# Decay times v as three wide bf16 matmuls per head, summed from three PSUM slots

## The chip, the cores and the metric

The kernel runs on one core of a Trainium2 chip. The metric is device time in microseconds, the median of several runs of one kernel. The profile is of one further execution, whose span runs from the first to the last instruction.

## The reference

An mLSTM over 4 batches, 8 heads, 768 steps and head size 40, followed by a gated feed-forward. For each batch and head:

```python
m_new = max(f + m, i);  f_stab = exp(f + m - m_new);  i_stab = exp(i - m_new)
C = f_stab * C + i_stab * outer(v, k);   n = f_stab * n + i_stab * k
h = C @ q;   y = sigmoid(o) * h / max(abs(n . q), 1)
```

and then, with `x` of shape 3072 x 320 and 1536 hidden columns: `out = (sigmoid(x @ w_gate) * (x @ w_val)) @ w_out`. All inputs and outputs are float32.

## The kernel before, in words

The 768 steps are cut into 6 chunks of 128. A **unit** is one chunk of one batch (8 heads), so there are 24 units, 4 to a chunk; chunk 2 begins with unit 8. In a unit, `d` is the 128 x 128 decay matrix of each head. The scores `s` (q times k, L753) are multiplied into it on VectorE (`t`, L872), so that `d` then holds decay times score. `av` (L931) multiplies it by `v`, to which a column of ones is added, so that 41 columns give the 40 outputs and the denominator. `in` (L914) gives the contribution of the carried state `cst`, scaled by `ti` (L919). `ad` (L946) adds the two in PSUM, `nd` (L951 to L953) makes the reciprocal of the denominator from the 41st column, `ns` (L957) multiplies by the output gate, `ro` (L962) divides, `tx` (L971) transposes in blocks, and `xw`, `xr` bounce the unit's rows through DRAM (`scx`) to `xf`, transposed. `xh` and `xl` (L1000, L1004) split them into a high and a low part, the input of the feed-forward. `cs`, `cm`, `cd`, `ca` carry the state on.

From chunk 2 on (`halved`), `d` and `v` are split into three bf16 parts each: the upper half of the float32 word (`top`), the upper half of the remainder, and the remainder of that. GpSimd makes them: `da`, `db` for `d` (L887, L891) and `va`, `vb` for `v` (L898, L902). `av` is six matmuls of 41 columns per head, for the six products that matter, all added into one PSUM tile of 8 x 41 columns.

The feed-forward of a chunk runs over 12 blocks of 128 hidden columns, some of them in two halves of two batches. Of a block, `u0`, `r0` fill one PSUM bank (gate) and `u1`, `r1` another (value); `th` (ScalarE), `gx` (VectorE, into the value's bank), `gh` (ScalarE) and `gl` (VectorE, L1097) make the product's high and low part; `dn` multiplies by `w_out`. The next block's `u1` needs the bank that `gl` reads.

PSUM has eight banks: two for the feed-forward's blocks, four for its outputs, and two (`pa`) that all attention tiles take in turn. The program order is a list written out by hand, `ORDER`: each engine, and the queue of SP that issues nearly all DMAs, does its instructions in the list's order.

The masks `bmask` and `cmask` (128 x 3 x 128 and 128 x 3 x 41) tell which rows belong to which of three stacked heads; `rmask` is one column of `bmask`.

Of the kernel before, what the change touches and what calls it, by code (L numbers as in the profile page):

```python
# [23 lines left out]
    'AV': 2,  # L24
# [7 lines left out]
    'AD': 1,  # L32
# [15 lines left out]
    i2 lf wdr0 li i3 wz tab wk0 war0 pz wk1 wk2 wk3 wdo0 ga i0 gm0 il sp0.0 lq2 i1 wdv0 gs0 wbr0 gb wao0 wbo0 lq0  # L48
    wav0 lk0 gc tap tac sp0.1 ee0.0 lk1 gm1 sp1.0 wco0 lq1 wcr0 ee0.1 kw0 lo0 tr0.1 wor0 whr0 wbv0 wlr0 gm2 lv0 i5
# [38 lines left out]
    gh23 u0.24 sh9.1 ns8 r0.24 th24 gl23 dn22.1 u1.24 r1.24 u0.25 nd8 r0.25 sl9.1 gx24 s9.2 th25 s9.1 cd8.1 t9.2
    gh24 dn23.0 s9.0 gl24 tw10.2 u0.26 tw10.0 ro8 r0.26 t9.0 tw10.3 u1.25 r1.25 ea10 t9.1 gx25 sq10.0 dn23.1 gh25
    cs8 tx8 th26 sr10.00 sr10.01 sr10.02 cm8.1 cm8.0 lk11 sr10.10 sr10.11 sr10.12 xw8.3 dn24.0 xw8.2 dn24.1 gl25  # L90
    u1.26 r1.26 gx26 lv10 u0.28 og9 r0.28 va9 dn25.1 gh26 vb9 ob0.2 dn25.0 th28 gl26 u1.28 r1.28 da9 gx28 lv11
    dn26.1 gh28 sh10.0 u0.27 r0.27 tq11 gl28 xw8.1 tw11.3 sl10.0 tw11.1 ca8.1 dn26.0 dn28.2 tw11.2 u1.27 r1.27 th27
    sh10.1 ee10 in9 gx27 tw11.0 db9 av9.0 av9.1 sq10.1 av9.2 sl10.1 u0.29 r0.29 ld11 dn28.3 gh27 gl27 cd8.0 ti9 l110
    va10 th29 ad9 nd9 sq11.0 ns9 u1.29 r1.29 l111 sq11.1 gx29 gh29 dn27.1 lo10 xw8.0 s10.2 u0.30 dn27.0 em10 kw10
    ro9 s10.0 t10.2 s10.1 sr11.00 sr11.01 sr11.02 sr11.10 sr11.12 r0.30 gl29 t10.1 dn29.2 t10.0 u1.30 th30 da10 db10
    r1.30 in10 u0.31 cd10.1 cd10.0 dn29.3 gx30 gh30 r0.31 th31 sr11.11 cs9 lk12 cm9.1 vb10 gl30 ca8.0 u1.31 r1.31
    gx31 dn30.2 gh31 ld12 gl31 dn30.3 og10 u0.32 tx9 xw9.0 xw9.1 xw9.2 r0.32 ti10 th32 sh11.0 xr8.0 u1.32 xr8.2
    r1.32 ea11 dn31.3 gx32 gh32 gl32 u0.34 dn31.2 r0.34 tq12 lq13 tw12.3 tw12.0 tw12.1 cm9.0 tw12.2 u1.34 lo11 xw9.3
    r1.34 dn32.3 th34 gx34 u0.33 va11 r0.33 dn32.2 ee11 em11 gh34 gl34 u1.33 sh11.1 r1.33 ob1.1 sl11.0 lv12 th33
    gx33 av10.0 ld13 sl11.1 av10.1 av10.2 u0.35 xr8.1 kw11 r0.35 gh33 cd9.1 og11 gl33 ad10 xr9.0 ns10 cd9.0 s11.2  # L100
    t11.2 dn33.3 dn33.2 nd10 u1.35 r1.35 s11.0 dn34.3 t11.0 lq15 vb11 th35 gx35 dn34.2 gh35 ro10 cs10 lk13 xr9.2
    s11.1 sr12.10 ca9.1 u0.36 sr12.00 ea12 r0.36 ee12 em12 cm10.1 th36 gl35 u1.36 ca9.0 t11.1 da11 tx10 xw10.1
    xw10.2 r1.36 xw10.3 xw10.0 db11 sr12.02 gx36 dn35.2 cm10.0 kw12 gh36 xr9.1 gl36 sq12.0 u0.37 r0.37 tq13 dn35.3
    dn36.3 u1.37 sr12.11 r1.37 sr12.01 in11 ca10.0 av11.0 av11.1 av11.2 th37 u0.38 gx37 gh37 sr12.12 gl37 ti11 ad11
    r0.38 u1.38 th38 r1.38 nd11 dn36.2 gx38 gh38 ns11 dn37.3 ea13 xh8 ro11 gl38 u0.39 r0.39 tw13.0 xh9 dn37.2 tw13.3
    tx11 xw11.3 xw11.2 xw11.0 xw11.1 u1.39 cd11.1 r1.39 xl8 xr10.0 xl9 xr10.2 th39 xr10.1 dn38.2 gx39 tw13.1 gh39
    gl39 dn38.3 u0.40 r0.40 lo12 ca10.1 xr11.0 sh12.0 dn39.3 sl12.0 u1.40 r1.40 tw13.2 xr11.2 dn39.2 xr11.1 th40
    gx40 sh12.1 ob1.3 gh40 u0.41 ob1.0 cs11 gl40 r0.41 th41 dn40.1 cm11.0 cm11.1 sl12.1 u1.41 r1.41 gx41 u0.42 r0.42
    s12.2 lo13 s12.1 l112 va12 ld14 gh41 gl41 th42 dn41.1 u1.42 r1.42 xh10 xl10 xh11 t12.2 gx42 s12.0 lq14 dn40.0
    dn41.0 gh42 xl11 vb12 ee13 og12 sq12.1 u0.43 r0.43 th43 lk14 og13 sr13.10 sr13.11 sq13.0 sr13.12 sq13.1 cd11.0  # L110
    t12.1 gl42 u1.43 r1.43 dn42.1 dn42.0 ob1.2 t12.0 da12 db12 gx43 gh43 gl43 u0.44 r0.44 u1.44 r1.44 th44 gx44
    dn43.2 u0.45 sr13.00 sr13.02 sr13.01 gh44 em13 r0.45 in12 av12.0 av12.1 sh13.1 kw13 tq14 tw14.1 av12.2 gl44
    u1.45 th45 ti12 dn44.2 cd12.0 tw14.3 r1.45 cd12.1 ca11.0 ad12 dn43.3 dn44.3 nd12 sl13.1 u0.46 r0.46 sh13.0 gx45
    ns12 in13 tw14.0 ld15 lv13 gh45 ca11.1 gl45 cs12 tw14.2 ro12 tx12 cd13.1 xw12.1 sl13.0 xw12.2 dn45.3 ti13 xw12.3
    cm12.0 u1.46 s13.2 cd13.0 t13.2 th46 lk15 r1.46 l113 gx46 dn45.2 xw12.0 cm12.1 sq14.0 s13.1 lv15 lv14 va13 vb13
    s13.0 sr14.00 sr14.01 sr14.02 sr14.10 sr14.11 gh46 l114 t13.1 t13.0 gl46 ca12.0 u0.47 r0.47 sr14.12 u1.47 r1.47
    ea15 ee15 cs13 lo15 sq14.1 th47 av13.0 gx47 gh47 ea14 dn46.0 ee14 ca12.1 gl47 cm13.0 ca13.0 dn46.1 tq15 lq17
    lk16 sh14.0 u0.48 r0.48 sl14.0 th48 dn46.2 dn47.2 em15 lo14 u1.48 sh14.1 u0.49 sl14.1 r1.48 r0.49 dn47.1 da13
    cm13.1 db13 ld16 lq16 tw15.0 dn46.3 tw15.1 dn47.3 dn47.0 tw15.2 gx48 s14.0 gh48 gl48 av13.1 av13.2 ad13 em14
    ns13 kw14 dn48.1 nd13 t14.0 u1.49 th49 ro13 tw15.3 tx13 ca13.1 l115 xr12.0 s14.2 ea16 ee16 dn48.2 dn48.0 s14.1  # L120
    sr15.10 t14.2 og14 r1.49 gx49 u0.50 r0.50 t14.1 gh49 sr15.12 gl49 sr15.00 og15 tq16 va15 sr15.11 in14 ti14 th50
# [1040 lines left out]
```

## Time and profile before

| | |
|---|---|
| runs | 518.97 us median of 3 (517.19 to 519.06) |
| profiled execution, span | 517.4 us, 1.6 us below that median |
| TensorE busy | 506.7 us, 4020 instructions |
| VectorE, ScalarE, GpSimd busy | 332.8, 242.1, 246.3 us |
| granted TensorE clock | 1.000 over the span |
| DMA | 74.17 MB, mean 143 GB/s |

The span is what the instructions take from the first to the last; a run's time is taken by the device around it. Matmuls are pipelined: a record's length is not its cost, and the cost of a row of equal matmuls is read from the chain of waits, which gives each piece the time that it adds.

### The profile page before, as it was taken

The numbers are of one execution on the slowest core, as the hardware profiler recorded it, in microseconds if no ns is written. First come the engines' busy times: TensorE is split into PE (matmuls) and PEld (weight loads), VectorE is DVE, ScalarE is ACT, GpSimd is POOL, SyncE is SP. The second block draws the span as 40 slices with busy tenths as digits, with TensorE's granted clock in tenths as the row PEclk, the third lists the DMA queues.
The fourth block names the chain that finished last, engine by engine and source line by source line (L and its number), as shares of the span: only waits on it lengthen the run. The fifth ranks groups of instructions, "written<-read, shape, count | busy, mean of one in ns | idle before, by whom it ended". The sixth has DMA issues, their size and how long they took to land.

```text
span 517.4 us, 11006 instructions
## 1 busy us (share of the span) xinstructions
PE 506.7 (98%) x4020; PEld 468.3 (91%) x4021; DVE 332.8 (64%) x699; ACT 242.1 (47%) x560; POOL 246.3 (48%) x272
## 2 busy tenths in 40 slices
PE   6989999999999999999999999999999999999997
PEld 4789988889999999998888888898888888999996
DVE  7978877785776677678766456856445474642332
ACT  4887766554444354644444443353344324232322
POOL 3656546557146686459536544187315504510000
PEclk9999999999999999999999999999999999999999
DMA  8999875339687797799879787599465835220000
GB/s 196 259 231 225 223 201 141 102 95 178 135 185 156 166 203 163 162 205 158 171 138 178 181 153 141 135 181 185 96 146 102 173 81 111 65 58 1 1 27 27
DMA packets 222478, 74.17 MB, mean 143 GB/s; under 512 B 167380, under 2 KB 214168, under 8 KB 222424
## 3 DMA queue, kind: packets, MB, share of 16 engines
q1 hardware_dynamic: 221336, 73.20, 64.8%
q8 instruction: 32, 0.52, 0.4%
q10 hardware_dynamic: 1088, 0.26, 0.2%
q14 instruction: 22, 0.18, 0.1%
HBM read 61.54 MB, written 11.90 MB: 142 GB/s over the span
## 4 chain that ended last, share of the span: by engine, by line
PE 89%; DMA 5%; ACT 2%; DVE 2%; issue 1%; SPq 1%; POOL 0%; POOLq 0%; DVEq 0%; ACTq 0%
PE pg L1070 38%; PE po L1107 8%; PE po L1109 8%; PE po L1108 7%; PE pg L1074 6%; PE pg L1075 6%; PE av L931 3%; PE s L753 2%; PE av L938 2%; DMA d<-mscr 2%; PE in L914 2%; PE cs L1014 2%; PE s L808 1%; DMA st_v<-in_moe_w_val_dram 1%; DMA scx<-tx 1%
## 5 line engine op out<-in xcount | busy, mean ns | idle before, releaser
L1092 ACT ACTIVATE gh<-pg 128x256 fp32r<-128x256 f32 (+1 forms) x103 | 48.2, 468 | 142.9 <-DVE pg L1087 120.7
L1087 DVE SCALAR_TENSOR_TENSOR pg<-sg,pg 128x256 f32<-128x256 f32 (+1 forms) x103 | 54.8, 532 | 92.1 <-PE pg L1075 75.4
L1070 PE MATMUL pg<-xh,wh 128*128 128x256 f32 (+1 forms) x412 | 104.8, 336 | 0.2 <-ACT xh L1000 0.2
L1070 PE MATMUL pg<-xh,wl 128*128 128x256 f32 (+1 forms) x412 | 100.9, 326 | 0.0
L1070 PE MATMUL pg<-xl,wh 128*128 128x256 f32 (+1 forms) x412 | 100.8, 326 | 0.0
L1107 PE MATMUL po<-oh,gh 128*128 128x320 f32 x288 | 92.6, 322 | 0.0
L1109 PE MATMUL po<-oh,gl 128*128 128x320 f32 x288 | 89.1, 309 | 0.1
L1108 PE MATMUL po<-ol,gh 128*128 128x320 f32 x288 | 88.9, 309 | 0.0
L1080 ACT ACTIVATE sg<-pg 128x256 f32<-128x256 f32 (+1 forms) x103 | 48.1, 467 | 73.3 <-PE pg L1075 71.9
L1097 DVE TENSOR_TENSOR gl<-pg,gh 128x256 fp32r<-128x256 f32 (+1 forms) x103 | 54.3, 527 | 36.6 <-ACT gh L1092 34.9
L1070 PEld LDWEIGHTS pg<-xl,wh 128*128 128x128 f32 x412 | 69.1, 189 | 7.3 <-POOL xl L1004 0.3
L1070 PEld LDWEIGHTS pg<-xh,wl 128*128 128x128 f32 x412 | 69.0, 189 | 7.1
L1070 PEld LDWEIGHTS pg<-xh,wh 128*128 128x128 f32 x412 | 67.7, 189 | 3.7 <-DVE gl L1097 0.6
L1074 PE MATMUL pg<-xh,w 128*128 128x256 f32 (+1 forms) x206 | 68.5, 333 | 0.0
L1075 PE MATMUL pg<-xl,w 128*128 128x256 f32 (+1 forms) x206 | 67.0, 326 | 0.0
L1107 PEld LDWEIGHTS po<-oh,gh 128*128 128x128 f32 x288 | 54.4, 189 | 2.5
L1108 PEld LDWEIGHTS po<-ol,gh 128*128 128x128 f32 x288 | 54.2, 188 | 2.6
L1109 PEld LDWEIGHTS po<-oh,gl 128*128 128x128 f32 x288 | 54.1, 188 | 0.7 <-DVE gl L1097 0.6
L671 POOL TENSOR_SCALAR_AFFINE_SELECT d<-d 128x1024 f32<-128x1024 f32 x22 | 26.2, 1192 | 52.6 <-ACT d L667 51.9
L887 POOL TENSOR_TENSOR dr<-d 128x1024 f32<-128x1024 f32 x16 | 30.3, 1894 | 35.7 <-DVE d L872 35.3
L872 DVE TENSOR_TENSOR d<-s,d 128x384 f32<-128x384 f32 (+2 forms) x68 | 34.9, 527 | 14.5 <-PE s L753 8.9
L1075 PEld LDWEIGHTS pg<-xl,w 128*128 128x128 f32 x206 | 39.0, 189 | 2.7
(159 smaller groups left out, 886.2 us busy)
## 6 DMA issues: line engine op xcount, KB each, us to landing
d<-mscr SPq DMA_DIRECT2D x22, 512.0 KB
ks<-scq SPq DMA_DIRECT2D x48, 168.0 KB
qs<-scq SPq DMA_DIRECT2D x48, 168.0 KB
scq<-tq SPq DMA_DIRECT2D x64, 80.0 KB
su_o<-in_moe_w_out_dram SPq DMA_DIRECT2D x12, 320.0 KB
o<-in_o_gate_dram SPq DMA_DIRECT2D x24, 160.0 KB
v<-in_v_dram SPq DMA_DIRECT2D x24, 160.0 KB
out_dram<-ob SPq DMA_DIRECT2D x24, 160.0 KB
```

Of the source, the lines that this page charges most:

```text
L872: nc.vector.tensor_tensor(y, ps_[n, g][:, :nh, :], y, ALU.mult)
L887: E("da", n).tensor_tensor(dr[n][0], dm[n], top(dm[n]), ALU.subtract)
L1070: nc.tensor.matmul(p, w[y][:, a, fs], x[c][:, a, n0:n1], start=(i + a == 0), stop=False)
L1074: nc.tensor.matmul(pg[n, y], w2[y][:, fs], xh[c][:, 2, n0:n1], start=False, stop=False)
L1075: nc.tensor.matmul(pg[n, y], w2[y][:, fs], xl[c][:, 2, n0:n1], start=False, stop=True)
L1080: nc.scalar.activation(s, pg[n, 0], AF.Tanh, scale=0.5)
L1087: nc.vector.scalar_tensor_tensor(sgs[n], gate, 1.0, pg[n, 1], ALU.add, ALU.mult)
L1092: nc.scalar.activation(ghs[n][:, :nt], sgs[n], AF.Copy)
L1097: E("gl", n).tensor_tensor(gls[n][:, :nt], sgs[n], ghs[n][:, :nt].bitcast(F32), ALU.subtract)
L1107: nc.tensor.matmul(p, ghs[n][:, ts], oh[:, j, :], start=(j == 0), stop=False)
L1108: nc.tensor.matmul(p, ghs[n][:, ts], ol[:, j, :], start=False, stop=False)
L1109: nc.tensor.matmul(p, gls[n][:, ts], oh[:, j, :], start=False, stop=(j == NF - 1))
```

## The change

From chunk 2 on, `v`'s three bf16 parts lie side by side in one tile `vs` (slots of 41 columns), and a head's product is three matmuls: the top of `d` times all three parts (123 columns), the last remainder of `d` times the first part (41), and the middle part of `d` times the first two (82). The slots stay apart in PSUM, so a unit's product is two tiles of four heads (`av{n}.0`, `av{n}.1`, one bank each), and VectorE adds the state's contribution and the three slots (`ad{n}.{half}{slot}`). `nd` and `ns` run for each half. A ScalarE copy `vc` puts the top of `v` into the tile; `va`, `vb` write into its other slots. Scores and their products go in two groups of four heads instead of 3, 3 and 2. The large masks are dropped for `rmask`, which is now made directly; the product with a mask reads it broadcast; `cd` scales all 120 rows of the state, whose unused rows `iz` clears at the start.

The order of feed-forward instructions on TensorE, ScalarE and VectorE is the same. SP's order is the same but for `ld16`, which now stands between the third and the last `tw` of unit 15, after four steps that stood behind it. Attention steps stand at other places, as here around the products of units 18 and 19:

```diff
-    ... u0.64 xr17.1 cm17.0 s19.2 t19.2 s19.1 t19.1
-    dn62.2 r0.64 gh63 db18 s19.0 t19.0 th64 av18.0 vb19 lo21 av18.1 av18.2 xr16.1 gl63 sr20.10 dn63.0 sr20.12 u1.64
-    r1.64 u0.65 da19 db19 ad18 r0.65 lq21 sr20.11 xh16 og19 cd18.0 nd18 ns18 ro18 in19 av19.0 av19.1 tx18 xw18.2
-    xw18.0 xw18.1 xw18.3 xl16 av19.2 ld20 dn63.1 gx64 gh64 th65 gl64 u1.65 r1.65 u0.66 r0.66 dn63.3 dn63.2 dn64.2
-    cd18.1 xh17 ti19 dn64.1 sr20.00 sr20.01 og21 sr20.02 cd17.1 dn64.3 xl17 ad19 nd19 ns19 ro19 tx19 gx65 gh65 th66
+    ... u0.64 s19.0 s19.1 xr17.1 db18 dn62.2 va18 vb18
+    cd18.1 r0.64 gh63 t19.0 av18.1 t19.1 th64 lo21 av18.0 xr16.1 gl63 vc19 sr20.10 dn63.0 sr20.12 va19 da19 u1.64
+    cd18.0 ad18.10 ad18.11 ad18.00 ad18.01 ad18.12 r1.64 ad18.02 u0.65 r0.65 nd18.1 ns18.1 lq21 nd18.0 ns18.0 ro18
+    sr20.11 xh16 tx18 in19 og19 xw18.2 xw18.0 xw18.1 vb19 xw18.3 db19 xl16 ld20 dn63.1 gx64 av19.0 ti19 gh64 th65
+    av19.1 gl64 u1.65 r1.65 u0.66 ad19.00 ad19.10 r0.66 dn63.3 cd17.1 ad19.01 ad19.11 dn63.2 dn64.2 ad19.12 ad19.02
+    xh17 ns19.0 dn64.1 sr20.00 sr20.01 og21 sr20.02 nd19.0 ns19.1 dn64.3 xl17 nd19.1 cs18 ro19 tx19 gx65 ca17.1 gh65
```

The code, cut to its core:

```diff
+FOURS = ((0, 4), (4, 4))
...
-    bmask = const.tile([P, 3, L], F32, name="bmask")
-    cmask = const.tile([P, 3, DA], F32, name="cmask")
-    ones = bmask[:BH, 0, :]
+    ones = rmask[:BH, 0:1].broadcast_to([BH, L])
...
+    @op("iz")
+    def _():
+        nc.gpsimd.memset(cst[64:, :, 2, : 2 * DA], 0.0)
...
-        block_mask(bmask, L)
+        block_mask(rmask.unsqueeze(2), 1)
...
-                for g, (h0, nh) in enumerate(GROUPS):
+                for g, (h0, nh) in enumerate(FOURS):
                     @op(f"s{n}.{g}")
...
+            @op(f"vc{n}")
+            def _():
+                vs[n] = sbt("su", [P, H, 3, DA], F32, f"vs_{n}", 2)
+                nc.scalar.activation(top(vs[n][:, :, 0, :]), top(vt[n]), AF.Copy)
...
-                E("va", n).tensor_tensor(vr[n][0], vt[n], top(vt[n]), ALU.subtract)
+                E("va", n).tensor_tensor(vs[n][:, :, 1, :], vt[n], top(vt[n]), ALU.subtract)
...
-            for i in range(3):
-                @op(f"av{n}.{i}")
-                def _(i=i):
-                    if i == 0:
-                        pv_[n] = pst(P_(f"av{n}"), [P, H, DA], f"av_{n}")
-                    dp = top(dm[n]) if i == 0 else top(dr[n][0]) if i == 1 else dr[n][1]
-                    vp = [top(vt[n])] if i == 2 else [top(vt[n]), top(vr[n][0]), vr[n][1]][: 3 - i]
-                    for h in range(H):
-                        for j, w in enumerate(vp):
-                            nc.tensor.matmul(pv_[n][:, h, :], dp[:, h, :], w[:, h, :], start=(i + j + h == 0),
-                                             stop=(i == 2 and h == H - 1))
+            for y in range(2):
+                @op(f"av{n}.{y}")
+                def _(y=y):
+                    pv_[n, y] = p = pst("pa", [P, 4, 3, DA], f"av_{n}_{y}")
+                    parts = vs[n].rearrange("p h j e -> p h (j e)").bitcast(BF16)
+                    for i, (dp, w) in enumerate(((top(dm[n]), 3 * DA), (dr[n][1], DA), (top(dr[n][0]), 2 * DA))):
+                        for x in range(4):
+                            nc.tensor.matmul(p.rearrange("p x j e -> p x (j e)")[:, x, :w], dp[:, 4 * y + x, :],
+                                             parts[:, 4 * y + x, 1 : 2 * w : 2], start=(i + x == 0), stop=(i + x == 5))
+
+                for i in range(3):
+                    @op(f"ad{n}.{y}{i}")
+                    def _(y=y, i=i):
+                        if n not in t1s:
+                            t1s[n] = sbt("t1", [P, H, DA], F32, f"t1_{n}", 2)
+                        t, p = t1s[n][:, 4 * y : 4 * y + 4, :], pv_[n, y][:, :, i, :]
+                        if c == 0 and i == 0:
+                            nc.scalar.activation(t, p, AF.Copy)
+                        else:
+                            nc.vector.tensor_tensor(p if i == 2 else t, t, p, ALU.add)
...
+        for y in range(2 if halved else 1):
+            hs = (lambda y=y: pv_[n, y][:, :, 2, :]) if halved else lambda: pv_[n]
+            heads = slice(4 * y, 4 * y + 4) if halved else slice(0, H)
```

## Rows read from the trace of the kernel before

**Rows 1.** The page's busy table: us busy, share of the span, instructions.
```profile
PE 506.7 (98%) x4020; PEld 468.3 (91%) x4021; DVE 332.8 (64%) x699; ACT 242.1 (47%) x560; POOL 246.3 (48%) x272
```

**Rows 2.** Busy time by stages: stretch, its length, each engine's us and instructions.
```profile
230.00:256.00 26.00, 25.97 (x188) 22.76 (x187) 21.22 (x34) 12.53 (x25) 18.58 (x19) 1.00 0.89 162
...
312.00:359.00 47.00, 46.87 (x423) 41.76 (x422) 33.98 (x65) 18.11 (x32) 27.25 (x26) 1.00 0.79 157
...
430.00:460.00 30.00, 30.00 (x291) 28.87 (x290) 17.18 (x37) 11.39 (x23) 12.24 (x11) 1.00 0.29 67
```

**Rows 3.** TensorE's waits from 300 us on: waiter, releaser, us, times, longest.
```profile
PE pg L1070 <- ACT xh L1000: 0.2, 1, 0.2
```

**Rows 4.** The chain of waits: start, us that it adds, work, matmuls.
```profile
262.33 1.21 PE av L931 x48
...
318.18 1.39 PE pg L1070 x6
...
332.86 0.29 PE s L753 x3
...
452.70 0.72 PE pg L1070 x6
```

**Rows 5.** Groups by line and shape, VectorE: count, busy us, mean ns, idle before.
```profile
L957 DVE SCALAR_TENSOR_TENSOR o<-o,av 128x320 f32<-128x320 f32 x24 | 11.2, 465 | 1.2 <-ACT o L906 0.4 <-PE av L938 0.4
L946 DVE TENSOR_TENSOR av<-t,av 128x328 f32<-128x328 f32 x20 | 10.0, 500 | 3.9 <-PE av L931 3.4 <-PE av L938 0.2
...
L872 DVE TENSOR_TENSOR d<-s,d 128x256 f32<-128x256 f32 x20 | 8.4, 419 | 6.8 <-PE s L753 5.5 <-PE s L808 1.2
...
L872 DVE TENSOR_TENSOR d<-s,d 128x512 f32<-128x512 f32 x8 | 5.1, 683 | 0.1
L953 DVE RECIPROCAL den<-den 128x8 f32<-128x8 f32 x24 | 4.9, 203 | 0.8
...
L952 DVE SCALAR_TENSOR_TENSOR den<-av,den 128x8 f32<-128x8 f32 x24 | 4.0, 166 | 0.8
...
L951 DVE TENSOR_SCALAR den<-av 128x8 f32<-128x8 f32 x24 | 3.8, 160 | 0.3
```

**Rows 6.** The same groups, ScalarE, the output gates.
```profile
L906 ACT ACTIVATE o<-o 128x320 f32<-128x320 f32 x24 | 10.9, 464 | 2.9 <-DMA o<-in_o_gate_dram 2.9
```

**Rows 7.** The same groups, GpSimd, the last remainder of the decay.
```profile
L891 POOL TENSOR_TENSOR ds<-dr 128x1024 bf16<-128x1024 f32 x16 | 30.6, 1915 | 0.9
```

**Rows 8.** Instructions in order of time from 0 us, VectorE's first scan.
```profile
3.42 0.45 DVE L409 TENSOR_TENSOR_SCAN gin<-bmask,gin 32x128 f32<-32x128 f32 x1 [0.56 <-DMA gin<-in_f_gate_dram]
```

**Rows 9.** The chain of waits into the start of chunk 4.
```profile
359.96 5.09 DMA scx<-tx
...
366.16 2.05 DMA xf<-scx
...
368.24 0.53 ACT xh L1000
...
368.81 1.83 PE pg L1070 x6
```

**Rows 10.** VectorE in order of time, 346 to 359 us: start, us, [idle before].
```profile
346.96 0.89 DVE L872 TENSOR_TENSOR d<-s,d 128x256 f32<-128x256 f32 x2 [1.73 <-PE s L753]
348.46 0.56 DVE L872 TENSOR_TENSOR d<-s,d 128x384 f32<-128x384 f32 x1 [0.61 <-PE s L753]
...
353.63 0.69 DVE L1097 TENSOR_TENSOR gl<-pg,gh 128x512 fp32r<-128x512 f32 x1 [0.67 <-ACT gh L1092]
...
355.72 0.50 DVE L946 TENSOR_TENSOR av<-t,av 128x328 f32<-128x328 f32 x1 [0.71 <-PE av L931]
...
357.78 0.51 DVE L971 STREAM_TRANSPOSE tx<-x 128x320 f32<-128x320 f32 x1
```

**Rows 11.** Groups by line and shape, TensorE's weight loads of scores and decay.
```profile
L753 PEld LDWEIGHTS s<-qs,ks 126*128 126x128 f32 x128 | 18.5, 190 | 1.3 <-DVE t L919 0.5
...
L931 PEld LDWEIGHTS <-d 128*128 128x128 bf16 x384 | 11.7, 98 | 0.4 <-issue 0.3
```

More of the change, by code (lines that the diff above doesn't have):

```diff
@@ L23 @@
     'V32': 1,
-    'AV': 2,
+    'AVN': 8,
     'EP': (),
@@ L88 @@
[L88 to L97, printed above, removed]
@@ new lines @@
+    ob1.0 gl40 r0.41 th41 dn40.1 sl12.1 u1.41 r1.41 gx41 cm11.0 u0.42 r0.42 lo13 s12.1 l112 ld14 gh41 gl41 th42
+    dn41.1 u1.42 r1.42 xh10 xl10 ca11.0 vc12 xh11 gx42 s12.0 lq14 dn40.0 dn41.0 gh42 xl11 t12.1 t12.0 ee13 og12
+    sq12.1 u0.43 va12 r0.43 th43 da12 lk14 og13 sr13.10 sr13.11 sq13.0 sr13.12 vb12 sq13.1 gl42 u1.43 ca11.1 db12
+    r1.43 dn42.1 dn42.0 in12 ob1.2 gx43 gh43 gl43 u0.44 r0.44 u1.44 r1.44 av12.0 th44 ti12 av12.1 gx44 dn43.2 u0.45
+    sr13.00 sr13.02 sr13.01 gh44 em13 r0.45 sh13.1 kw13 tq14 tw14.1 gl44 u1.45 ad12.00 ad12.10 ad12.01 cd12.0
@@ L560, in mlstm_then_gated_ffn_kernel @@
     pt_, ps_, pi_, pv_, px_, pc_, pm_ = {}, {}, {}, {}, {}, {}, {}
-    split, vr, dr, stk, sgn, tx, xf = {}, {}, {}, {}, {}, {}, {}
+    split, vs, dr, stk, sgn, tx, xf = {}, {}, {}, {}, {}, {}, {}
     POPEN = {
@@ L798, in _ @@
                 @op(f"qb{n}.{g}")
-                def _(g=g, nh=nh, r=r):
+                def _(g=g, h0=h0, nh=nh, r=r):
                     qkt, qbd = sop[n]
-                    E(f"qb{g}", n).tensor_tensor(qbd[:r, g, :nh, :], qkt[:r, g, 0, :].unsqueeze(1).broadcast_to([r, nh, L]),
-                                                 bmask[:r, :nh, :], ALU.mult)
+                    E(f"qb{g}", n).tensor_tensor(qbd[:r, h0 : h0 + nh, :], qkt[:r, g, 0, :].unsqueeze(1).broadcast_to([r, nh, L]),
+                                                 rmask[:r, :nh].unsqueeze(2).broadcast_to([r, nh, L]), ALU.mult)
                 @op(f"s{n}.{g}")
-                def _(g=g, nh=nh, r=r):
+                def _(g=g, h0=h0, nh=nh, r=r):
                     qkt, qbd = sop[n]
                     ps_[n, g] = p = pst(P_(f"s{n}.{g}"), [P, 3, L], f"s_{n}_{g}")
-                    nc.tensor.matmul(p[:, :nh, :], qkt[:r, g, 1, :], qbd[:r, g, :nh, :], start=True, stop=True)
+                    nc.tensor.matmul(p[:, :nh, :], qkt[:r, g, 1, :], qbd[:r, h0 : h0 + nh, :], start=True, stop=True)
         else:
@@ L866, in _ @@
                                               sc[:, 0, :, x, :].rearrange("m d w -> d m w"))
-        for g, (h0, nh) in enumerate(((0, 4), (1, 4)) if padded or paired else GROUPS):
+        for g, (h0, nh) in enumerate(((0, 4), (1, 4)) if padded or paired else FOURS if bounced else GROUPS):
             @op(f"t{n}.{g}")
@@ L938, in _ @@
                     nc.tensor.matmul(p[:, h, :], dm[n][:, h, :], vt[n][:, h, :], start=True, stop=True)
-        def hs():
-            return t1s[n] if c > 0 and not PARAM["AD"] else pv_[n]
-        if c > 0:
+        if c > 0 and not halved:
             @op(f"ad{n}")
             def _():
-                nc.vector.tensor_tensor(hs(), t1s[n], pv_[n], ALU.add)
-        @op(f"nd{n}")
-        def _():
-            rden[n] = den = sbt("den", [P, H], F32, f"den_{n}", 2)
-            nc.vector.tensor_scalar(den, hs()[:, :, D], -2.0, 2.0, ALU.mult, ALU.max)
-            nc.vector.scalar_tensor_tensor(den, hs()[:, :, D], 2.0, den, ALU.mult, ALU.max)
-            nc.vector.reciprocal(den, den)
-        @op(f"ns{n}")
-        def _():
-            nc.vector.scalar_tensor_tensor(ot[n], ot[n], 1.0, hs()[:, :, :D], ALU.add, ALU.mult)
+                nc.vector.tensor_tensor(pv_[n], t1s[n], pv_[n], ALU.add)
+        for y in range(2 if halved else 1):
+            hs = (lambda y=y: pv_[n, y][:, :, 2, :]) if halved else lambda: pv_[n]
+            heads = slice(4 * y, 4 * y + 4) if halved else slice(0, H)
+            yn = f"{n}.{y}" if halved else f"{n}"
+            @op(f"nd{yn}")
+            def _(hs=hs, heads=heads):
+                if n not in rden:
+                    rden[n] = sbt("den", [P, H], F32, f"den_{n}", 2)
+                den = rden[n][:, heads]
+                nc.vector.tensor_scalar(den, hs()[:, :, D], -2.0, 2.0, ALU.mult, ALU.max)
+                nc.vector.scalar_tensor_tensor(den, hs()[:, :, D], 2.0, den, ALU.mult, ALU.max)
+                nc.vector.reciprocal(den, den)
+            @op(f"ns{yn}")
+            def _(hs=hs, heads=heads):
+                o = ot[n][:, heads, :]
+                nc.vector.scalar_tensor_tensor(o, o, 1.0, hs()[:, :, :D], ALU.add, ALU.mult)
         @op(f"ro{n}")
@@ L1039, in _ @@
                 tmps[y] = tmp
-                if is_act("cm", n):
-                    for j in range(w // DA):
-                        js = slice(j * DA, (j + 1) * DA)
-                        nc.scalar.activation(tmp[:, :, js], pc_[n][:r, gs, js], AF.Copy, scale=rmask[:r, j : j + 1])
-                else:
-                    cm = cmask.rearrange("p j e -> p (j e)")[:r, :w].unsqueeze(1).broadcast_to([r, ng, w])
-                    nc.vector.tensor_tensor(tmp, pc_[n][:r, gs, :w], cm, ALU.mult)
+                for j in range(w // DA):
+                    js = slice(j * DA, (j + 1) * DA)
+                    nc.scalar.activation(tmp[:, :, js], pc_[n][:r, gs, js], AF.Copy, scale=rmask[:r, j : j + 1])
             if c > 0:
```

220 lines of the change are left out of this document (111 added, 109 removed).

## The prediction

> **What bounds the kernel now.** I read the page's busy table first: TensorE is busy 506.7 us, 98% of the span of 517.4 us [rows 1]. So the time is TensorE's own work plus the places where it waits. The table by stages comes next, because the change loads VectorE: VectorE is busy 21.22 of 26.00 us at 230 to 256 us and 33.98 of 47.00 us at 312 to 359 us, while TensorE has next to no idle time in either [rows 2]. The third view, TensorE's waits, has a single one after 300 us: the first matmul of a chunk waited for `xh` [rows 3]. The chain of waits shows where that one comes from, and I return to it below. A TensorE microsecond saved therefore shows only as long as no such wait takes it back.
>
> The profiled execution spans 517.4 us and the timed runs have a median of 518.97 us (517.19 to 519.06), 1.6 us above it. I sum against the span and move the median by the result.
>
> **The change, part by part.** Sixteen units (8 to 23, chunks 2 to 5) change.
>
> *Matmuls of decay times v.* A unit issues 48 bf16 matmuls of 41 columns now. The chain gives 1.21 us for the 48 of one unit, 25.2 ns each [rows 4]. After the change it issues 24: per head one of 123 columns, one of 82 and one of 41. The column count is the same (8 x 246 = 48 x 41 = 1968), so only what a matmul costs beyond its columns can go. Six 512-column matmuls take 1.39 us and six 256-column ones 0.72 us [rows 4], which is 232 and 120 ns each, so 0.436 ns a column and 8 ns fixed. With the fixed part, 123 columns cost 62 ns and 82 cost 44; without it 54 and 36. The 41-column one keeps 25. A head costs 115 to 131 ns against 6 x 25.2 = 151, so 20 to 36 ns are saved. I take the middle, 28 ns: 8 heads give 0.225 us a unit, 16 units 3.6 us, with ends 2.6 and 4.6 us.
>
> The Trainium skill ("TensorE: Matmul & The Clock Gate", Wait — 56ns, not 53.3ns?) states that spacing never falls below about 25 ns however few the columns, and is columns / 2.4 plus 2.5 ns otherwise; the 25.2 ns row agrees. By that rule 123, 82 and 41 columns cost 54, 37 and 25 ns, which is the upper end of the saving, 4.6 us.
>
> *VectorE's sums.* Each half unit of four heads now holds three slots, and VectorE adds them: six adds of 164 elements in place of one of 328. The `d<-s,d` rows give 683 ns at 512 elements and 419 at 256 [rows 5], so 1.03 ns an element and 155 ns fixed; 164 elements take 324 ns. Six are 1.94 us against 0.500 for the one [rows 5]: +1.44 us. The denominators run twice, 160 + 166 + 203 = 529 ns more [rows 5]. The scaling with the output gate is split in two, 465 ns becoming 2 x 0.31: +0.16 us. The score products go from three (384, 384, 256 elements: 0.55 + 0.55 + 0.42) to two of 512 (2 x 0.68): -0.15 us. Together VectorE gets +2.0 us a unit, 32 us in all, on an engine that is not the bottleneck. It costs nothing where VectorE has idle time. Where it has none it delays the residual `gl`, which TensorE needs before the next value matmul, and `tx`, which starts the transfers to the feed-forward input. With two units at 230 to 256 us VectorE would be at about 25 of 26 us, and with four at 312 to 359 us at 42 of 47 us [rows 2].
>
> *The hidden edits.* ScalarE gets one copy of 328 elements a unit, about 0.46 us by the 320-element `o` row [rows 6], 7.4 us over 16 units on an engine busy 47% [rows 1]. If it lost its cover, at most 0.46 us a unit would pass into the sums. The product now needs both remainders before it can end its second third, while now only the last sixth of it needs them. GpSimd makes each in 1.9 us [rows 7], and the list puts them earlier; uncovered, that is up to 1.9 us a unit, covered zero, and GpSimd is busy 48% [rows 1], so I take zero. The smaller mask shortens GpSimd's first microseconds by some 1 us, but the scan behind it was released by the DMA of the forget gates at 3.42 us [rows 8]: zero, or -0.5 us if that was close. The added memset of the state stands on GpSimd in the same stretch, behind the mask that became shorter. The transfer of the decay rows of unit 16 passes behind four small ones in SP's queue, and GpSimd's step on them now follows close behind it, with the remainders of unit 14 queued after that: zero if the landing is hidden, at the most the 5.1 us of a landing [rows 9] for unit 14, some 100 us before the wait at chunk 4, which would swallow it. TensorE has one group of scores fewer and one of products more a unit: zero.
>
> *Where the saving is taken back.* Chunk 4 of the feed-forward starts at 368.81 us with the wait named above. It needs the activations of unit 19. Their chain: `tx` of unit 19 on VectorE ends at 357.78 + 0.51 = 358.29 us [rows 10]; then the bounce through DRAM lands 5.09 us of `scx`, 2.05 us of `xf`, and ScalarE copies for 0.53 us [rows 9]. That is 10.5 us that TensorE cannot shorten. Before `tx`, VectorE ran from the scores of unit 19 at 346.96 us with waits of 0.61, 0.67 and 0.71 us inside, 11.33 us in all [rows 10]. The change puts the added work of two units into just this stretch: 2 x 2.1 us less the 0.15 of the scores, +4.1 us. If the waits close completely it takes 11.33 - 2.0 + 4.1 = 13.4 us, if not 15.4 us. TensorE's lead when it hands over these scores is that of ten units, 2.25 us, so `tx` of unit 19 would end at 346.96 - 2.25 + 13.4 = 358.1 us, or 360.1. I take 358.1, since every input of the adds is there by then and VectorE runs without a break: the start of chunk 4 moves by -0.2 us (at the other end +1.8). TensorE would arrive 12 x 0.225 = 2.7 us earlier than now and wait for it. Of the lead of units 8 to 19 about 0.2 us survives. Chunk 4 on keeps the saving of four units, 0.9 us, as VectorE has room there: 17.18 of 30.00 us at 430 to 460 us [rows 2].
>
> **Sum.** -0.2 - 0.9 = -1.1 us: 516.3 us on the span, 517.9 us against the median.
>
> **The rivals.**
>
> *The lead survives.* If VectorE's queue before the scores of unit 19 empties earlier too, or the landing of `scx` depends on the backlog in the DMA queue and not on `tx`, chunk 4 starts with TensorE and nothing is taken back: -3.6 us, 515.4 us. For it: VectorE stood idle 1.73 us before those scores [rows 10], and the feed-forward order that all of this hangs on is the same. Against it: the waits inside the chain add up to only 2 us, the work put in to 4.
>
> *VectorE becomes the bound, slower.* In the two dense stretches its load rises to 90% and more. It takes its instructions in order, so an add that waits for the product keeps `gx` and `gl` behind it, and TensorE stops before the value matmul. In the profile gl followed gx by 0.67 us of waiting for ScalarE [rows 10]; once that gap is gone, what remains of 2.0 us is TensorE's wait. At 0.6 us for each of the 12 units in chunks 2 to 4 that is 7.2 us, less the 3.6 saved and the 0.2 of the junction that then absorbs it: about +3.4 us, 522.4 us. It eats the whole saving from 0.3 us a unit on (12 x 0.3 = 3.6).
>
> *The wide matmuls pay for their weight loads.* If a new load could not run beside the matmul before it, 123 columns would cost what scores do, three in 0.29 us or 97 ns for 128 columns [rows 4]. A head then costs 97 + 65 + 25 = 187 ns, 36 more than now: +4.6 us, 523.6 us. Against it: the loads of scores are recorded at 190 ns, those of the decay at 98 [rows 11], and 41-column matmuls with a load each run at 25.2 ns. The Trainium skill ("TensorE: Matmul & The Clock Gate", Back-to-back issue gap) gives about 81 ns at 128 columns in a stream of load and matmul; by it a head costs some 155 ns and the saving is nil. No row here shows it for bf16.
>
> **How the numbers follow.** A timed difference under 0.5% (2.6 us) is what a measurement of this kernel cannot tell from no change. Saving mostly taken back at chunk 4: 0.48. Lead survives: 0.30. VectorE the bound: 0.15. Loads paid: 0.07. The first case's own range is 516.7 to 519.9 us, from a 4.6 us saving of which half is kept to the late end of `tx` (+1.8 - 0.9). The second is all faster, and a little of the first: 0.33. The last two are slower but for the part where the extra is under 2.6 us: 0.19. Same: 0.48. The range for 8 in 10 reaches from the 4.6 us end, 514.3, to 522 us.
>
> **What would show it.** Right: a unit's products take about 0.99 us in place of 1.21; VectorE's busy total rises from 332.8 [rows 1] to about 365 us; the wait before chunk 4 grows to between 2 and 3 us with `xh` as releaser, and TensorE has no idle time elsewhere. Wrong: chunk 4 starts near 365 us with no wait (the lead survives); waits of value matmuls on `gl` scattered through 220 to 360 us (VectorE the bound); a unit's products at 1.3 us or more (the loads).

## The result, and the profile after

The changed kernel takes 523.44 us (median of 11 runs, 521.39 to 527.39) against 519.06 us for the kernel before on the same chip (517.19 to 522.75). The ratio is 1.0082, 95% interval 1.0056 to 1.0109: slower by 0.8%, 4.3 us. Times below are such ratios times 519 us, each against the kernel before, run in turn with it. The profiled span went from 517.4 to 521.7 us, +4.3 as well.

The page's busy table, against [rows 1]:

```profile
PE 509.4 (98%) x3636; PEld 465.5 (89%) x3637; DVE 347.1 (67%) x827; ACT 249.9 (48%) x576; POOL 243.2 (47%) x269
```

TensorE has 384 instructions less and, by the lengths of its records, is busy 2.7 us more: what it saved came back as time spent waiting inside the matmuls and between them. By stages, against [rows 2]:

```profile
230.00:256.00 26.00, 24.99 (x158) 21.51 (x157) 18.21 (x39) 12.77 (x25) 16.46 (x15) 1.00 0.98 174
312.00:359.00 47.00, 47.00 (x326) 41.37 (x325) 37.61 (x87) 21.14 (x40) 28.57 (x27) 1.00 0.79 144
430.00:460.00 30.00, 30.00 (x236) 28.15 (x236) 18.86 (x44) 10.81 (x21) 15.71 (x13) 1.00 0.42 100
```

The surprise is the first line. From 230 to 256 us TensorE now stands idle for 1.0 us, and VectorE, which was to be near 25 of 26 us, is busy for only 18.21. It waits too (and not all of the same steps fall into the stretch, since TensorE runs 1.4 to 4 us later there). In the second stretch VectorE got its work (37.61 us for 33.98) and TensorE lost nothing.

TensorE's waits from 300 us on, against [rows 3], hold no `xh` any more; from 140 to 470 us there are these:

```profile
PE pg L1084 <- DVE gl L1111: 1.7, 2, 1.0
PE av L932 <- ACT ct L1060: 0.9, 1, 0.9
PE po L1123 <- DVE gl L1111: 0.3, 2, 0.2
PE s L753 <- PE pg L1089: 0.3, 1, 0.3
```

All but 0.2 us of it lies before 300 us. The feed-forward's matmuls, whose order is the same, can be compared start by start: TensorE is 0.0 us behind the kernel before at 121 us, 2.8 at 208, 1.4 at 241 and 4.5 at 293. After that the number moves between 2.5 and 5.5, since attention steps stand at other places, and it is 4.3 from 470 us to the end. So chunk 4's start took nothing back. The product saves 3.6 us over sixteen units, eight of them on each side of 293 us: of the 7.9 us lost in all, some 6.3 are lost before 293 us and 1.6 after.

The products themselves did what was forecast. The chain of waits has 24 matmuls in 1.01 us where [rows 4] has 48 in 1.21:

```profile
320.47 1.01 PE av L932 x24
```

VectorE's new groups, against [rows 5] (count, busy us, mean ns, idle before):

```profile
L872 DVE TENSOR_TENSOR d<-s,d 128x512 f32<-128x512 f32 x40 | 26.2, 682 | 2.9 <-PE s L753 2.8
...
L944 DVE TENSOR_TENSOR t<-t,av 128x164 f32<-128x164 f32 x64 | 18.8, 317 | 4.8 <-PE av L932 4.2
...
L944 DVE TENSOR_TENSOR av<-t,av 128x164 f32<-128x164 f32 x32 | 9.8, 327 | 0.2
...
L974 DVE SCALAR_TENSOR_TENSOR o<-o,av 128x160 f32<-128x160 f32 x32 | 9.4, 307 | 0.2
```

The longest wait comes about like this. ScalarE's copy `gh` stands in its queue behind a copy of score operands that had waited 3.40 us for a transfer, and TensorE waits for the residual behind it (ScalarE, then TensorE, in order of time):

```profile
285.04 1.15 ACT L727 ACTIVATE qt<-qs,rsign 126x1024 fp32r<-126x1024 f32 x1 [3.40 <-DMA qs<-scq]
286.10 0.58 ACT L1106 ACTIVATE gh<-pg 128x512 fp32r<-128x512 f32 x1
...
287.46 0.73 PE L1084 MATMUL pg<-xh,wh 128*128 128x512 f32 x2 [0.99 <-DVE gl L1111]
```

### The profile page after: what moved, and what is told of

Read it like the earlier page. It is cut to its first block, busy times and chain, and to the rows that moved or that the text cites. A ratio compares the mean times of both kernels' runs of the same rounds, so it can differ in the third digit from the quotient of the medians.

```text
span 521.7 us, 10381 instructions
## 1 busy us (share of the span) xinstructions
PE 509.4 (98%) x3636; PEld 465.5 (89%) x3637; DVE 347.1 (67%) x827; ACT 249.9 (48%) x576; POOL 243.2 (47%) x269
## 4 chain that ended last, share of the span: by engine, by line
PE 72%; DMA 13%; SPq 4%; ACT 4%; DVE 4%; issue 2%; POOL 0%; DVEq 0%; ACTq 0%
PE pg L1084 31%; PE po L1121 7%; PE po L1123 7%; PE po L1122 6%; PE pg L1088 5%; PE pg L1089 5%; DMA ks<-scq 3%; DMA qs<-scq 3%; PE s L753 2%; PE av L932 2%; PE in L917 2%; DMA st_g<-in_moe_w_gate_dram 2%; PE av L950 2%; PE cs L1031 1%; DMA d<-mscr 1%
## 5 line engine op out<-in xcount | busy, mean ns | idle before, releaser
L1084 PE MATMUL pg<-xh,wh 128*128 128x256 f32 (+1 forms) x412 | 106.3, 339 | 1.9 <-DVE gl L1111 1.7
L1088 PEld LDWEIGHTS pg<-xh,w 128*128 128x128 f32 x206 | 38.9, 189 | 2.8
```

Source lines behind the costliest of these rows:

```text
L1084: nc.tensor.matmul(p, w[y][:, a, fs], x[c][:, a, n0:n1], start=(i + a == 0), stop=False)
L1088: nc.tensor.matmul(pg[n, y], w2[y][:, fs], xh[c][:, 2, n0:n1], start=False, stop=False)
```

## The experiments

My theory after reading the two traces was VectorE's added work; the rival was the list, which moves some steps of each unit whatever the product costs. The runs have short names (e1, e2 and so on), by which the last sections call them.

**First four: the change in halves.** The old product in the new list:

```
 av{n}.{y}:  for i, dp in enumerate((top(dm), top(dr), ds)): for h in half y: for j in range(3 - i):
                 matmul(pv[:, h, :], dp[:, h, :], vp[j][:, h, :])     # one slot, 41 columns
 ad, nd, ns: once a unit, on 8 heads
```

> The changed kernel with the old product in units 8 to 23: 48 matmuls of 41 columns into one slot, half of the heads at each of the two places where the wide ones stood, one add, one set of denominators and one scaling a unit, no copy of the top halves of v; the changed order, the scores in two groups of four and the small masks stay. TensorE gets the 3.6 us of products back, VectorE loses about 29 us of work (96 adds of 0.32 us become 16 of 0.50, and so on). Theory 'VectorE's work': the waits of the changed kernel come from VectorE's added work, so without it the time is that of the kernel before, 518 to 520.5 us. Rival 'the order': the steps that were moved put VectorE and ScalarE behind late transfers and behind GpSimd, whatever the product costs; then the 7.9 us of waits stay and the 3.6 us come on top: 525 to 528 us.

Measured (e1): 1.0116 (1.0073 to 1.0159), +6.0 us. The list, with the scores by four and the other small edits that the run keeps, costs as much without the wide product as with it.

The new product in the old list (`av n.0`, `av n.1` at the place of `av n.2`, six `ad` at that of `ad`, `vc` before `va`):

> The other half: the wide product with its six adds, two sets of denominators and two scalings, in the order of the kernel before (wide matmuls at the place of the last of the three old steps, the adds at the place of the one add, the copy of v's top halves just before its first remainder); scores in three groups as before; a few steps moved behind their releasers where two PSUM banks are now held. Theory 'VectorE's work': as late as the changed kernel or later, since the order does not make room for the adds: 523 to 527 us. Rival 'the order': without the moved steps only TensorE's saving is left: 515 to 517 us.

Measured (e2): 1.0665 (1.0636 to 1.0695), +34.5 us. Both theories are too small here. The old list can't take the product as it stands.

The changed kernel with `if i == 2:` in front of the add (the sums then hold the third slot only):

> The changed kernel without the adds of the first two slots (four of six a unit, 64 in all, 0.317 us each: 20 us of VectorE's work), so the second and third parts of the sums are left out; all else stays. Theory 'VectorE's work': 20 of the 29 us of added work are gone, and with them most of the waits of 7.9 us; TensorE keeps its 3.6 us: 516 to 519 us. Rival 'the order': the waits stay: 522 to 524.5 us.

Measured (e3): 1.0046 (1.0016 to 1.0077), +2.4 us. Twenty microseconds of VectorE's work are worth 1.9 us by the medians (the interval overlaps that of the changed kernel), and the kernel is still no faster than before, with 3.6 us less on TensorE.

The changed kernel with `for j in range(nj)` around matmuls of 41 columns:

> The changed kernel with each wide matmul cut into matmuls of 41 columns that write the same three slots: 48 a unit again, everything else as in the changed kernel. It gives back TensorE's saving of 3.6 us and nothing else. If TensorE's saving reaches the end of the kernel undiminished: 526 to 528 us. If the path runs through VectorE in the stretches where the waits are, part of it is hidden in those waits: 523.5 to 526 us.

Measured (e4): 1.0119 (1.0088 to 1.0150), +6.2 us, 1.9 more than the changed kernel. The intervals of the two overlap, so the run does not tell how much of the 3.6 us came back.

**Mending the list.** A control first, the kernel before once more:

> The kernel before, profiled once more, as a control for what one profile can carry. If the median of a 512-column matmul is 230 to 231 ns again and the span is within 1.5 us of 517.4, the 233 ns that the changed kernels show is theirs; if it is 233 ns here too, some 2 us between two profiles say nothing of the kernels.

Measured (g1): span 517.6 us, median matmul of 512 columns 231 ns from start to start between 60 and 140 us, where the changed kernel has 233. The 2 ns are the changed kernel's (e1 has them too), but over the 361 such matmuls between 300 and 470 us they make under 1 us. What makes them is not shown; the product cannot, since it has not changed yet at 60 to 140 us.

Entries moved at six places (`sl10.1`, `tx9`, `s11.0`, `ca12.1 cm13.1 cm13.0`, `sh16.0`, `xh18`, eight in all and not ten, and nothing else):

> The changed kernel with ten entries of its list moved and nothing else, at six places where its trace shows TensorE waiting: the second low part of unit 10's scores behind gl27; tx9 behind gl30; s11.0 to just before s11.1; cm13 (with the add before it) ahead of sh14.1; sh16.0 behind gh53; xh18 behind gh66. The waits at these places are 0.40, 0.98, 0.44, 1.02 with 0.42 behind it, 1.26 and 0.70 us: 5.2 us. Theory 'the order': each is an instruction that stands in front of the one that TensorE needs, in the queue of an engine that takes them in order, so moving it takes the wait away: 518 to 520 us. Rival 'VectorE's work': the waits come back at the next instruction, since the work is still there: 522 to 524 us.

Measured (g2): 1.0096 (1.0062 to 1.0130), +5.0 us. Nothing gained. The six waits are gone or smaller and others stand next to them: scores wait 0.97 us until 173.66 us, and on VectorE the very `sl10.1` that I put later (1.54 us, to 172.64) stands in front of the scaling `ns9.1`, which ends just ahead of them at 173.56 us; an output matmul at 253 us waits 1.29 us for `gh`. What sets the waits that only moved, this run does not show.

The mended list with two slots (`pst("pa", [P, 4, 2, DA])`, matmuls of 82, 41, 82, 41 columns):

> The mended list, and the product in two slots for three: per head one matmul of 82 columns (top of the decay times first and second part of v), one of 41 (lowest decay part times first part), one of 82 (middle part times first and second) and one of 41 (top times third), so four adds a unit for six. VectorE loses 32 adds of 0.32 us, 10.2 us; TensorE gets 4 matmuls of 39 + 25 + 39 + 25 = 128 ns a head for 124 (60 + 39 + 25), 0.5 us in all. By the run without four adds (20 us less work gave 1.9 us) it is worth 1.0 less 0.5 us: 0.5 us under the mended list. If VectorE's work were what holds TensorE, it would be 2 us or more under it.

Measured (g3): 1.0146 (1.0118 to 1.0174), +7.6 us. Less work on VectorE and a longer time by the medians (the intervals just overlap): the expectation missed by 3 us on the wrong side. At 190 us, for one, two instructions of VectorE took 1.86 and 1.43 us beside GpSimd's where the mended kernel has 1.39 and 1.28. Why it lost so much in all stays open.

Scores by four in the kernel before (`GROUPS` becomes `FOURS` in `s` and `t`):

> The kernel before with one part of the change alone: from chunk 2 on its scores and their products with the decay go in two groups of four heads for three of 3, 3 and 2 (two of the three steps of the old list keep their place). Theory 'the order': grouping costs nothing, 518.5 to 520.5 us. Rival 'the groups': four heads in a bank hold it longer and a product of 512 elements stands longer on VectorE, and a part of the 6 us that the order alone costs is this: 521.5 us or more.

Measured (g4): 1.0031 (1.0012 to 1.0050), +1.6 us. On the edge between the two theories; a small price, but not zero.

**Buffers and transfers.** In the changed kernel, `sbt("bl" or "bh", ..., 2)` and `sbt("d", ..., 4)`:

> The changed kernel with a second buffer for each of the two operands of the scores and a fourth for the decay, list unchanged. To make room, the low parts of the feed-forward weights are computed as before but not kept, and TensorE reads the high parts in their place (same matmuls, same tiles' sizes). Theory 'the loop' (the scores of a unit must end before the next unit's operands may land, and transfer, copies, low parts and scores take nearly all of a unit's 18.8 us): the transfers start up to 0.8 us earlier a unit where the queue already waits for the scores, so 1 to 3 us less than the changed kernel: 520.5 to 522.5 us. Theory 'the list alone' (the list sets each queue's order, and buffers don't matter): 522.5 to 524 us.

Measured (h1): 1.0052 (1.0030 to 1.0073), +2.7 us, 1.6 less than the changed kernel by the medians; the intervals overlap, so a gain is not shown. The rows of unit 16, which the last part of this section follows, leave no earlier than in the changed kernel (251.88 us for 250.63), so the fourth buffer did nothing there.

The same with `sr` and `sq` about four steps earlier in the list, in the changed kernel and in the one before:

> The same, and in the list the transfers that fetch the operands of scores and of the state's product stand some four steps of the feed-forward earlier (3 us), not ahead of the transfers they read from. Theory 'the loop': the landing is out of the way, ScalarE no longer waits in front of gh, and what the product saves shows: 515.5 to 518.5 us. Theory 'the list alone': the waits stay elsewhere, 522 to 524.5 us.

> The kernel before with the same second buffers and the same earlier transfers, as a control. TensorE has no wait to lose here, so both theories say 518 to 520 us; above 521 us would mean that the earlier transfers themselves disturb the others.

Measured (h2, h3): 1.0392 (1.0355 to 1.0429) and 1.0341 (1.0300 to 1.0382). Both are 18 to 20 us slower, the control too, so they say nothing on the buffers. From h1, h2 differs by the list alone and is 17.6 us slower: transfers moved ahead in an ordered queue can cost far more than they gain. What they held up was not followed.

**What in the list costs it.** Three runs on the kernel before:

```
 i1:  av{n}.0 av{n}.1 moved to stand with av{n}.2
 i2:  ad{n}:  for _ in range(4): tensor_tensor(scratch, t1s[n][:, :4], pv[n][:, :4], ADD)    # before the add
 i3:  the new product in the old list, ad only for i == 2
```

> The kernel before with one thing moved in its list: the first two thirds of a unit's 48 matmuls of decay times v stand where the last third stands, behind both remainders, as the wide product has to. Same instructions on every engine. Theory 'the early start': the first third used to run while GpSimd still made the remainders, gave the scores' PSUM bank back sooner and let go of the decay's buffer; without it units end later: 522 to 526 us, most of what the changed list costs. Theory 'the list alone': the start of the product is of no weight, 518.5 to 520.5 us.

> The kernel before with four more adds of 164 elements in front of each unit's one add from unit 8 on, into a scratch tile that nothing reads: 64 adds of 0.32 us, 20 us of VectorE's work, the same that was taken out of the changed kernel for 1.9 us. Theory 'VectorE's work': it costs as much or more here, where the list made no room for it, 521 to 523 us. If VectorE has the room: 518.5 to 520 us.

> The wide product in the old order (554.9 us), without the adds of the first two slots (the sums lack these parts): 20 us of VectorE's work less. If the adds, standing in VectorE's queue in front of gx and gl, are what costs 35 us there: 530 us or less. If it is the two PSUM banks and the late start of the product: 545 to 553 us.

Measured: i1 1.0021 (0.9999 to 1.0043), +1.1 us, not told from zero by the times; i2 1.0329 (1.0308 to 1.0351), +17.1 us; i3 1.0491 (1.0463 to 1.0519), 9 us less than with all adds. So 64 adds are worth 17.1 us in front of the old product's sum, 9 with the wide product in the old list and 1.9 in the new list.

Is that their amount or their place? The same adds between `gx` and `gl`, where VectorE waits for ScalarE:

```
 gl{n}:  for _ in range({256-column step: 1, 512-column step: 2}.get(n)): tensor_tensor(scratch, scratch, sgs[n][:, :164], ADD)
```

> The kernel before with adds of 164 elements into the same scratch tile, but placed between gx and gl, in steps of the feed-forward where VectorE has nothing else to do while ScalarE makes gh (0.45 us at 256 columns, 0.7 us at 512): one in 9 steps of 256 columns and two in 21 of 512, all between the products of units 8 and 23, 51 adds in all, 16 us of VectorE's work. At the rate of the adds in front of a unit's sum (17.1 us for 64) they would cost 13.6 us: 530 to 534 us if the amount decides. If the place decides: 519 to 522 us.

Measured (i4): 1.0094 (1.0058 to 1.0129), +4.9 us for 51 adds, 0.10 us each where i2 paid 0.27. Place decides most of it. In the profiled executions one event, shown in the last section, makes TensorE 4.8 us late in i4 and 5.9 in i2; without it i2's adds would still cost more than i4's.

Both parts that cost a little alone, together (`FOURS` and `av` at once):

> The kernel before with both parts: scores in two groups of four, and all 48 matmuls of a unit's product behind both remainders. If the parts add up, 2.7 us: 522 to 523.5 us, and some 3 us of what the changed list costs are left to the other moved steps. If the two feed each other (a bank held longer, a product that starts later): 525 us or more, and the list has no other price.

Measured (i6): 1.0080 (1.0050 to 1.0111), +4.2 us. These two steps alone, on the old product and the old list, cost what the whole change costs. They do not lose it at the same places: at 202 us TensorE is 0.1 us behind the kernel before in i6, 2.6 in the changed kernel and 3.5 in e1 (1.0 of it from before 121 us).

And the same two kernels with `sbt("d", ..., 4)`:

> The kernel with the product at once (i1), and a fourth buffer for the decay; for its room the low parts of the feed-forward weights are not kept and TensorE reads the high parts in their place. Theory 'the decay's buffer': the rows of unit 16 are issued before 247 us again, gh near 252 to 256 us is no later than before, and the span falls from 519.0 to 517.5 to 518 us (time 518.5 to 519.8). If the buffer isn't the cause: gh at 257 us as in i1, span 519 us.

> The kernel with both parts (i6) and the fourth buffer. Theory 'the decay's buffer': the part of the 4.2 us that hangs on it, some 2 us, goes, and the rest, which is the scores by four, stays: 521 to 522.5 us. If the buffer isn't the cause: 523 to 524.5 us.

Measured: i7 0.9992 (0.9974 to 1.0010), i8 1.0021 (1.0004 to 1.0038). By the medians the price of i1 is gone and 3.1 of the 4.2 us of i6; the intervals of i6 and i8 don't overlap, those of i1 and i7 do. What is left of i8, 1.1 us, is about the scores by four (1.6). No run makes the room without the fourth buffer, so the times alone don't tell the two apart. The traces show the way it goes. Transfer of the decay rows of unit 16, GpSimd's step on them, then ScalarE's queue, in the kernel before:

```profile
246.33 0.64 SPq L650 DMA_DIRECT2D d<-mscr  x1
...
251.28 1.90 POOL L663 TENSOR_TENSOR d<-at,d 128x1024 f32<-128x1024 f32 x1 [5.19 <-DMA d<-mscr]
...
253.21 1.06 ACT L667 ACTIVATE d<-d 128x1024 f32<-128x1024 f32 x1 [2.98 <-POOL d L663]
...
255.19 0.60 ACT L1092 ACTIVATE gh<-pg 128x512 fp32r<-128x512 f32 x1 [0.56 <-DVE pg L1087]
```

with both parts (i6):

```profile
250.47 0.34 SPq L644 DMA_DIRECT2D d<-mscr  x1
...
254.56 1.90 POOL L657 TENSOR_TENSOR d<-at,d 128x1024 f32<-128x1024 f32 x1 [4.83 <-DMA d<-mscr]
...
256.49 1.06 ACT L661 ACTIVATE d<-d 128x1024 f32<-128x1024 f32 x1 [5.62 <-POOL d L657]
...
257.82 0.58 ACT L1086 ACTIVATE gh<-pg 128x512 fp32r<-128x512 f32 x1
```

and with the fourth buffer (i8):

```profile
246.52 0.85 SPq L644 DMA_DIRECT2D d<-mscr  x1
...
252.20 2.24 POOL L657 TENSOR_TENSOR d<-at,d 128x1024 f32<-128x1024 f32 x1 [5.26 <-DMA d<-mscr]
...
254.47 1.06 ACT L661 ACTIVATE d<-d 128x1024 f32<-128x1024 f32 x1 [4.00 <-POOL d L657]
...
255.80 0.58 ACT L1086 ACTIVATE gh<-pg 128x512 fp32r<-128x512 f32 x1
```

The transfer queue's own waits from 244 to 264 us say what held the transfer up, in i6 and, longer, with the wide product in the old list (e2):

```profile
SPq L644 <- PE av L925: 3.4, 1, 3.4
...
SPq L647 <- PE av L929: 7.0, 1, 7.0
```

The kernel before and i8 have no such wait. Three buffers hold the decay, so unit 16 needs that of unit 13. In the kernel before, the first of the three steps of unit 13's product (24 of its 48 matmuls, the only ones that read the decay itself) starts at 239.53 us, while GpSimd still makes the remainders. In i6 it starts 10.1 us later. The rows of unit 16 are then issued 4.1 us later, GpSimd and ScalarE follow, and `gh`, behind the exponential in ScalarE's queue, comes at 257.82 in place of 255.19 us. TensorE waits for that one at once: against the kernel before it falls behind by 1.0 us at 257 us in i6 and by 0.9 in i1, and by nothing there in i8 and i7. So the buffer is the cause at this place. (The room by itself gains nothing earlier: from 60 to 230 us TensorE in i7 keeps its distance from the kernel before to 0.1 us.) It does not account for all of the 3.1 us: the two profiled executions are 1.4 us apart in span, and that of i7, one of its slowest (521.6 us, where 517.5 to 518 was expected), has waits of 1.0 us at 237 and 0.3 us at 249 us.

The changed kernel does not take this way. Its rows of unit 16 leave as late as in i6:

```profile
250.63 0.46 SPq L650 DMA_DIRECT2D d<-mscr  x1
...
258.66 0.58 ACT L1106 ACTIVATE gh<-pg 128x512 fp32r<-128x512 f32 x1
```

But its queue has no wait for the product there, nor has that of e1: three transfers of `tq`, which the new list puts in front, run without a break until 250.52 us. TensorE, by then over 3 us late, does not fall further behind at `gh`. Its waits near this place are for `ct` at 249.60 us (0.86 us) and for `gl` at 287.46 us (0.99 us), each behind a ScalarE copy of score operands that had waited for its transfer (1.02 and 3.40 us).

## Why the prediction was wrong

The forecast was 517.9 us, no change. The time is 523.44, on the other side of the kernel before and above the range, which ended at 522.

- **TensorE's saving: right.** Sized at 3.6 us. The products' start-to-start times sum to 19.7 us before and 17.1 after, which includes one wait of 1.0 us: 3.6 us. Medians are 60, 39 and 25 ns for 123, 82 and 41 columns. The Trainium skill ("TensorE: Matmul & The Clock Gate", Back-to-back issue gap), by which the saving would be nil, is not borne out: 123 columns with a load each run at 60 ns. The rival of paid loads (97 ns) falls.
- **The hidden edits: the step that failed.** The sum takes the moved steps at zero: the remainders ("so I take zero"), scores by four, the transfer of unit 16's rows; for the other moves it has no term. Run with the old product (e1) these edits cost 6.0 us (3.8 to 8.3), more than the 3.6 saved. On the old list two of them cost 4.2 us together. I had asked who waits for the remainders and not what the product's early start let go of: on the old list its delay makes the queue wait 3.4 us for the decay's buffer. In the changed list no such wait is left, so the price there comes about otherwise. Which of the moved steps makes the 2.6 us lost by 202 us, and which the rest, stays open; of the three longest waits that are seen, two stand behind ScalarE's copies of score operands, and moving entries at the places of the waits (g2) gained nothing. Unit 16's rows, which I said chunk 4 would swallow, left 4.3 us later, and TensorE did not wait for them.
- **VectorE: sized about right, placed wrong.** The new groups are as forecast (317 and 327 ns an add for 324), some 29 us more work in all for 32. VectorE's busy total rose by only 14.3 us: some 8 us less went to the sum into the state and the division, which were held up less (one division of 0.49 us took 2.69 at 322 us in the kernel before, beside two instructions of GpSimd's), and about 8 us is records that overlap. The two dense stretches are 70% and 80% busy, not 90%, and TensorE's 1.0 us of idle time in the first is mostly a wait for ScalarE's `ct`.
- **The junction at chunk 4: wrong.** No wait for `xh` of more than 0.1 us, where 2 to 3 were forecast. `tx` of unit 19 ended at 363.75 us, not near 358.1, and `xh` at 372.89, just ahead of TensorE's start at 372.94: both came late together, and nothing was left to take back.
- **The rivals.** "VectorE becomes the bound", 522.4 us, is nearest, by luck: waits on `gl` add up to 2.0 us, 20 us less work gave back 1.9, and without the wide product's adds (e1) the kernel is no faster. "The lead survives" did not occur.
- **The sum as far as the runs go.** The edits of e1 6.0 us, the wide product with its adds -1.7 (changed kernel less e1, with intervals that overlap): 4.3. That two steps on the old list cost as much (4.2) is a coincidence of amounts, since TensorE loses the time at other places.

## What to carry over

Before an instruction is merged with a later one, ask what its early start released: the buffer it reads, the transfer that waits for that buffer, and whose queue stands behind that transfer. When a change comes with a new order, price the order by itself: the old work in the new list. In a list that fills one engine to 98% the same work has no fixed price: 16 to 20 us more of VectorE's cost 2 to 17 us by place, so an engine's share of busy time does not say what more work on it costs. And a cause found in one list has to be looked for again in the other: two kernels can lose the same time at different places, and comparing starts shows where.

## What the runs showed of the hardware

In i4 a two-input instruction of VectorE on SBUF, 1.28 us elsewhere, took 4.54 us while GpSimd ran four instructions without a break. VectorE, then GpSimd, then TensorE:

```profile
190.72 4.54 DVE L733 SCALAR_TENSOR_TENSOR ks<-ks,rsign,kt 126x1024 fp32r<-126x1024 f32 x1
190.76 0.88 POOL L1025 TENSOR_TENSOR cst<-cst,cdec 80x82 f32<-80x82 f32 x2
191.59 0.73 POOL L902 TENSOR_TENSOR vr<-vr 128x328 bf16<-128x328 f32 x1
192.28 1.89 POOL L663 TENSOR_TENSOR d<-at,d 128x1024 f32<-128x1024 f32 x1
...
195.36 0.66 PE L753 MATMUL s<-qs,ks 126*128 126x128 f32 x2 [2.81 <-issue]
```

It ended 1.1 us after GpSimd's last one, about its own length. In the kernel before the same two instructions met with nearly the same starts (0.05 us apart for 0.04), and it was GpSimd's pair that was slow, 1.96 us for 0.88:

```profile
189.35 1.28 DVE L733 SCALAR_TENSOR_TENSOR ks<-ks,rsign,kt 126x1024 fp32r<-126x1024 f32 x1
...
189.40 1.96 POOL L1025 TENSOR_TENSOR cst<-cst,cdec 80x82 f32<-80x82 f32 x2
```

In i4 TensorE, waiting for VectorE's, lost 2.8 us, and then ran at a lower granted clock (length, TensorE, its loads, VectorE, ScalarE, GpSimd, clock):

```profile
188.00:192.00 4.00, 4.00 (x71) 3.83 (x70) 3.48 (x5) 2.33 (x5) 3.92 (x5) 1.00 0.99 179
192.00:196.00 4.00, 1.19 (x8) 1.01 (x7) 4.00 (x3) 0.85 (x2) 2.18 (x2) 0.92 0.97 248
196.00:200.00 4.00, 4.00 (x23) 4.00 (x23) 1.76 (x8) 0.00 (x0) 0.00 (x0) 0.66 0.12 22
```

A granted clock of 0.66 over 4 us is a mix of its two levels, 1.2 GHz for about two thirds of them and 2.4 for the rest; output matmuls of 147 ns took 270 in the slow part. The event made TensorE 4.8 us late, and i2 has the same one (4.41 us). The Trainium skill ("SBUF — State Buffer", Who interferes with whom) says that a VectorE instruction with two SBUF inputs contends with a GpSimd instruction that reads SBUF, and states: "Issue order, not op shape, decides who blocks." The traces agree on the contention (4.54 for 1.28 us, 1.96 for 0.88). On the order they don't settle it: VectorE's recorded start is ahead by 0.04 to 0.05 us both times, and it kept its length in one and lost to four instructions in a row in the other.
